# An attention and hard-swish kernel with its weight load moved behind x, some of batch 0's work moved off GpSimd, and a new table of operations

## The chip, the cores and the metric

The kernel runs on one core of one Trainium2 chip. The metric is the device time of a run in microseconds. Five engines take part: TensorE (PE; its weight loads are listed as PEld), VectorE (DVE), ScalarE (ACT), GpSimd (POOL) and SyncE (SP), which here only issues DMAs. Each works through its own list of instructions in order, and waits where an instruction's inputs or its target are not ready.

## The reference

```python
def mab(q, kv):
    s = scale * (q @ kv.transpose(0, 2, 1))
    s = s - s.max(-1, keepdims=True)
    a = np.exp(s)
    a /= a.sum(-1, keepdims=True) + 1e-09
    return a @ kv
h = mab(I, x)            # I: 32 inducing rows, the same for each batch
y = mab(x, h)            # x: 4 x 12480 x 128
...
h = y @ w_in             # 128 x 2048
relu6 = np.clip(h + 3.0, 0.0, 6.0)
return (h * relu6 / 6.0) @ w_out   # 2048 x 128
```

Each batch has two stages. In the first, 32 inducing rows attend over all 12480 rows of x. The second can only begin when that sum over the batch is complete: each row of x attends over the 32 results, and the outcome goes through the two-layer block.

## The kernel before, in words

A batch has six groups of 2048 rows (group numbers 0 to 5; 16 tiles of 128) and a rest of 192 rows (group 6). Everything that the engines do is written out in one string, `ORDER`: a table of 1625 operations, which the loop at L809 turns into calls of the functions `op_...`, one after the other. There is no scheduler behind it: the order of the table, read for one engine, is that engine's list. An entry is a code and its arguments, with the batch and the group first, then tiles or halves, then the PSUM bank (0 to 7), then the engine (V, A, P) where there is a choice. `X.1.2.0.16` loads tiles 0 to 16 of batch 1's group 2.

First stage, for each group: X loads x (1 MB, L422, issued on POOL's queue, into one of five buffers `xr`, so that it waits until the group five before is done with); K casts four tiles to bf16 (L426, four K a group, on ScalarE or VectorE); T transposes eight tiles on TensorE (L432) and Y copies them out of PSUM (L438, VectorE); S makes the logits (L443), E their exponential (L451, ScalarE), A the sum weighted by them (L459, TensorE), H adds it up in `hacc` (L470, L472) and D the denominators in `dacc` (L477, L479).

Between the stages, once a batch: c1 and c2 reduce the denominators (L483, L489), c3 sums them over the partitions with the matrix `ones` (L498, L499), c4 inverts, c5 transposes, c6 writes `HT` (L509); cA and cB make `dH` from it (L529, L532), c7 and c8 a rounded part and its remainder, c9 the two tables `HTs` and `Wd` that the second stage's logits need (L523 to L526). Then comes the two-layer block, evaluated through tables made from the 32 rows and not for each row of x: M multiplies by `w_hi` (L538, 16 times), N squares (L546 on ScalarE; L548 and L549 where it is VectorE's), P multiplies by `w_ob` (L601), G makes the 32 rows exactly with `w_hi` and `w_lo` (L555), cH to cJ, L (L578), cL to cN and cP leave two tables, `BD` and `Cq`.

Second stage, for each group: Z makes the logits, two products into two banks (L624; `Z.b.g.k1.k2` puts the differences in k1 and the logits in k2); Zd and Ze take their exponentials (L634, L639, ScalarE), W spreads one of them over the partitions by DMA (L645, SP's queue); R sums (L653), Rl takes the logarithm (L658, ScalarE), Rz subtracts (L663, VectorE; it reads the logits' bank k2 again), Ra is the exponential of that (L677, ScalarE), Rh a copy in fp16 (L688). Then, for each half group, B expands it into banks 0 to 3 (L696), F takes the exponential of two banks at a time (L706, ScalarE, two F a half), U multiplies (L717, VectorE). For each four tiles l and q sum the result in one of the banks 5 to 7 (L726, L743), v copies it out (L754, VectorE), O stores it (L763, SP's queue).

The weights: wi loads w_in whole (L399), wh rounds a quarter of it to bf16 (`w_hi`, L409), wl subtracts for the remainder (`w_lo`, L412), wo loads w_out (L402, POOL's queue) and wb rounds a quarter of it (`w_ob`, L415). Small things at the start: it loads ScalarE's table of functions, i1 makes the identity (POOL), i6, i7 and i9 are memsets and small copies on POOL (`ones`, `blk`, masks), w.n.k makes n matmuls on zeros (L359). At the end, yb and y0 to y5 compare a few sums with what they must be and leave one flag, which L813 reads; the branch behind it is not taken with these inputs.

The second stage of a batch runs beside the first stage of the next one, interleaved entry by entry in `ORDER`.

Of the kernel before, what the change touches and what calls it, by code (L numbers as in the profile page):

```python
# [28 lines left out]
K.0.2.12.16.V wl.2.P T.0.2.0.8.0 E.0.1.0.16.4 T.0.2.8.16.1 Y.0.2.0.8.0.V A.0.1.0.8.4 wl.3.P D.0.1.V A.0.1.8.16.4
Y.0.2.8.16.1.V S.0.2.0.8.0 K.0.3.0.4.A X.1.0.0.16 H.0.1.4 K.0.3.8.12.A S.0.2.8.16.0 K.0.3.4.8.V K.0.3.12.16.V  # L30
E.0.2.0.16.0 T.0.3.0.8.4 T.0.3.8.16.1 D.0.2.V A.0.2.0.8.0 Y.0.3.0.8.4.V A.0.2.8.16.0 Y.0.3.8.16.1.V S.0.3.0.8.4
K.0.4.0.4.A X.1.1.0.16 H.0.2.0 K.0.4.8.12.A S.0.3.8.16.4 K.0.4.4.8.V K.0.4.12.16.V E.0.3.0.16.4 T.0.4.0.8.0
K.0.6.0.2.A A.0.3.0.8.4 D.0.3.V A.0.3.8.16.4 Y.0.4.0.8.0.V T.0.4.8.16.1 X.1.2.0.16 H.0.3.4 S.0.4.0.8.0 Y.0.4.8.16.1.V
K.0.5.0.4.A T.0.6.0.2.4 K.0.5.8.12.A K.0.5.4.8.V S.0.4.8.16.0 K.0.5.12.16.V T.0.5.0.8.1 E.0.4.0.16.0 Y.0.6.0.2.4.V
T.0.5.8.16.2 Y.0.5.0.8.1.V A.0.4.0.8.4 D.0.4.V A.0.4.8.16.4 Y.0.5.8.16.2.V S.0.5.0.8.1 X.1.3.0.16 S.0.6.0.2.0
E.0.6.0.2.0 H.0.4.4 S.0.5.8.16.1 wb.0.P c2.0.- A.0.6.0.2.4 E.0.5.0.16.1 wb.1.P A.0.5.0.8.1 D.0.5.V wb.2.P A.0.5.8.16.1
wb.3.P c1.0.- X.1.4.0.16 H.0.5.1 c3.0.0 H.0.6.4 c5.0.4 c4.0.0 K.1.0.0.4.A c6.0.4 cA.0.V c7.0.A c9.0.P K.1.0.4.8.A
cB.0.V c8.0.P Z.0.0.4.0 K.1.0.8.12.V K.1.0.12.16.V M.0.0.1 Ze.0.0.0 M.0.1.2 M.0.2.3 N.0.0.1.A N.0.1.2.V Zd.0.0.4
M.0.3.1 N.0.2.3.A R.0.0.4 W.0.0 K.1.1.8.12.V N.0.3.1.A M.0.4.2 K.1.1.12.16.V G.0.0.3 N.0.4.2.A M.0.5.1 G.0.1.3
Rl.0.0.4 N.0.5.1.V M.0.6.2 G.0.2.3 K.1.1.0.4.A M.0.7.4 N.0.6.2.A G.0.3.3 Rz.0.0.0 N.0.7.4.A M.0.8.1 M.0.9.2 N.0.8.1.A  # L40
cH.0.3 P.0.0.4 P.0.1.4 Ra.0.0 M.0.10.0 N.0.9.2.V P.0.2.4 M.0.11.1 N.0.10.0.A P.0.3.4 P.0.4.4 N.0.11.1.A M.0.12.0
P.0.5.4 K.1.1.4.8.A cI.0.3 M.0.13.1 P.0.6.4 N.0.12.0.A M.0.14.2 cJ.0.3 P.0.7.4 N.0.14.2.A M.0.15.0 N.0.13.1.V P.0.8.4
N.0.15.0.A L.0.0.3 P.0.9.4 L.0.1.3 Rh.0.0.V P.0.10.4 cL.0.3 P.0.11.4 P.0.12.4 cM.0.3 P.0.13.4 cN.0.3 P.0.14.4 P.0.15.4
# [35 lines left out]
v.0.5.2.7.V B.1.0.0 q.0.5.3.0.6 cL.1.4 F.1.0.0.0 cM.1.4 F.1.0.0.1 q.0.5.3.1.6 cN.1.4 Z.1.1.0.1 v.0.5.3.6.V T.2.0.0.8.4
Ze.1.1.1 U.1.0.0.2 O.0.5.0.16 l.0.6.0.5 Zd.1.1.0 R.1.1.2 q.0.6.0.0.5 q.0.6.0.1.5 Rl.1.1.2 Y.2.0.0.8.4.V l.1.0.0.7  # L80
q.1.0.0.0.7 Rz.1.1.1 T.2.0.8.16.4 Rh.1.1.V B.1.0.1 Ra.1.1 Y.2.0.8.16.4.V q.1.0.0.1.7 F.1.0.1.0 v.0.6.0.5.V W.1.1
S.2.0.0.8.4 v.1.0.0.7.V S.2.0.8.16.4 l.1.0.1.6 F.1.0.1.1 K.2.2.8.12.V q.1.0.1.0.6 K.2.2.12.16.V q.1.0.1.1.6
# [119 lines left out]
def kernel(  # L202
# [31 lines left out]
    with ExitStack() as es:  # L234
# [53 lines left out]
        w_st = os_[NOS - 1]  # L288
# [109 lines left out]
        def op_wi(e):  # L398
            nc.sync.dma_start(w_st[:, :, :].rearrange("p a c -> p (a c)"), moe_w_in[:, :])  # L399
# [566 lines left out]
```

## Time and profile before

| | us |
|---|---|
| median of 3 runs (lowest, highest) | 324.18 (323.92, 326.12) |
| the profiled execution, its own time | 325.27 |
| its span in the profile | 323.5 |
| mean granted clock of TensorE | 0.94 |

Busy time in that span: TensorE 286.2 us, its weight loads 216.9, VectorE 246.6, ScalarE 225.9, GpSimd 61.0. Time in the rows that follow is counted from the span's start. A row of the timeline has the start, the length, the engine, the line in the kernel, the instruction, output and input, how many in a row, and in brackets how long the engine stood idle before and what ended that. A row of the table of windows has, for one stretch, its length, each engine's busy time with the number of its instructions in brackets, then TensorE's granted clock, the mean busy share of the DMA engines and their GB/s. Matmuls are pipelined, so TensorE counts as busy in part of the time in which it only waits for the next one.

### The profile page before, as it was taken

The numbers are of one execution on the slowest core, as the hardware profiler recorded it, in microseconds if no ns is written. First come the engines' busy times: TensorE is split into PE (matmuls) and PEld (weight loads), VectorE is DVE, ScalarE is ACT, GpSimd is POOL, SyncE is SP. The second block draws the span as 40 slices with busy tenths as digits, with TensorE's granted clock in tenths as the row PEclk, the third lists the DMA queues.
The fourth block names the chain that finished last, engine by engine and source line by source line (L and its number), as shares of the span: only waits on it lengthen the run. The fifth ranks groups of instructions, "written<-read, shape, count | busy, mean of one in ns | idle before, by whom it ended". The sixth has DMA issues, their size and how long they took to land. (4 is left out here: it accounts for less than half of the span.)

```text
span 323.5 us, 9751 instructions
## 1 busy us (share of the span) xinstructions
PE 286.2 (88%) x4101; PEld 216.9 (67%) x4101; DVE 246.6 (76%) x457; ACT 225.9 (70%) x387; POOL 61.0 (19%) x96
## 2 busy tenths in 40 slices
PE   5768399999989999999999998999989996989860
PEld 2567257778767777877877677787767763766640
DVE  2799777999798569889896589999875664877560
ACT  1733286979868788898788789866778677677620
POOL 8452500224221000532420003131110000000000
PEclk9589669999999999999999999999999997899795
DMA  7999820688998047789993338761653248167361
GB/s 235 428 385 363 296 67 3 181 239 237 339 340 308 5 162 232 223 303 344 271 321 135 138 83 257 275 191 28 193 180 138 66 149 256 25 200 219 148 234 56
DMA packets 23462, 66.74 MB, mean 206 GB/s; under 512 B 3664, under 2 KB 16752, under 8 KB 17264
## 3 DMA queue, kind: packets, MB, share of 16 engines
q1 hardware_dynamic: 19216, 39.41, 37.3%
q0 software_dynamic: 4192, 26.61, 24.1%
q8 instruction: 34, 0.56, 0.7%
q14 instruction: 20, 0.16, 0.2%
HBM read 27.67 MB, written 25.56 MB: 165 GB/s over the span
## 5 line engine op out<-in xcount | busy, mean ns | idle before, releaser
L706 ACT ACTIVATE TF<-ps 128x1024 bf16<-128x1024 f32 (+1 forms) x100 | 95.0, 999 | 26.6 <-PE ps L696 26.2
L754 DVE COPY os<-ps 128x512 f32<-128x512 f32 x96 | 64.7, 682 | 16.7 <-PE ps L743 16.3
L717 DVE TENSOR_TENSOR TD<-TF,d 128x2048 bf16<-128x2048 bf16 (+1 forms) x52 | 60.0, 1156 | 13.0 <-ACT TF L706 11.4
L743 PE MATMUL ps<-Cq,TD 128*128 128x128 bf16 (+1 forms) x784 | 60.6, 223 | 1.5 <-DVE TD L717 1.5
L743 PE MATMUL ps<-Cq,TF 128*128 128x128 bf16 (+1 forms) x784 | 61.6, 224 | 0.0
L743 PEld LDWEIGHTS <-TF 128*128 128x128 bf16 (+1 forms) x784 | 46.9, 101 | 14.9 <-issue 11.5
L743 PEld LDWEIGHTS <-TD 128*128 128x128 bf16 (+1 forms) x784 | 48.1, 101 | 7.2 <-issue 3.1
L726 PE MATMUL ps<-BD,a 128*128 128x512 f32 (+1 forms) x100 | 44.4, 462 | 2.0 <-DVE os L754 1.8
L438 DVE COPY xT<-ps 128x1024 bf16<-128x1024 bf16 x48 | 32.6, 683 | 4.6 <-PE ps L432 4.3
L432 PE MATMUL ps<-ident_b,xb 128*128 128x128 bf16 x384 | 30.5, 227 | 6.0 <-ACT xb L426 3.4
L546 ACT ACTIVATE sq<-ps 128x512 bf16<-128x512 f32 x60 | 32.3, 616 | 2.0 <-PE ps L538 1.8
L426 ACT CAST xb<-xr 128x512 bf16<-128x512 f32 x48 | 28.3, 627 | 6.1 <-DMA xr<-in_x_dram 6.1
L479 POOL TENSOR_TENSOR dacc<-dacc,a 128x512 f32<-128x512 f32 x15 | 21.2, 1414 | 59.1 <-ACT a L451 55.3
L432 PEld LDWEIGHTS <-xb 128*128 128x128 bf16 x384 | 24.0, 101 | 11.2 <-issue 4.4
L459 PE MATMUL ps<-xr,a 128*32 128x128 f32 x384 | 29.1, 228 | 2.2 <-ACT a L451 1.5
L459 PEld LDWEIGHTS ps<-xr,a 128*32 128x32 f32 x384 | 24.6, 111 | 4.8 <-ACT a L451 3.5
L426 DVE CAST xb<-xr 128x512 bf16<-128x512 f32 x48 | 24.8, 542 | 3.2 <-DMA xr<-in_x_dram 3.2
L677 ACT ACTIVATE a<-zz 128x512 fp32r<-128x512 f32 (+1 forms) x28 | 16.2, 579 | 14.5 <-DVE z_all L663 11.9
L696 PE MATMUL ps<-z,pair 32*128 32x256 f16 (+1 forms) x400 | 21.7, 275 | 4.2 <-ACT TF L706 2.8
L451 ACT ACTIVATE a<-ps 128x512 fp32r<-128x512 f32 x24 | 14.4, 599 | 14.3 <-PE ps L443 13.3
L726 PEld LDWEIGHTS ps<-BD,a 128*128 128x128 f32 (+1 forms) x100 | 18.0, 188 | 7.2 <-issue 2.6
L538 PE MATMUL ps<-dH,w_hi 128*128 128x512 bf16 x64 | 22.4, 404 | 0.0
(130 smaller groups left out, 371.7 us busy)
## 6 DMA issues: line engine op xcount, KB each, us to landing
xr<-in_x_dram POOLq DMA_DIRECT2D x23, 1024.0 KB, 7.4
out_dram<-os SPq DMA_DIRECT2D x23, 1024.0 KB, 4.8
d<-dk SPq DMA_DIRECT2D x96, 128.0 KB, 3.0
os<-in_moe_w_in_dram SPq DMA_DIRECT2D x1, 1024.0 KB, 4.9
xr<-in_x_dram POOLq DMA_DIRECT2D x2, 512.0 KB, 7.2
w_or<-in_moe_w_out_dram POOLq DMA_DIRECT2D x1, 1024.0 KB, 9.6
out_dram<-os SPq DMA_DIRECT2D x2, 512.0 KB, 4.4
xl<-in_x_dram POOLq DMA_DIRECT2D x4, 96.0 KB, 6.5
```

The lines of the kernel that those rows point to most:

```text
L426: copier(e)(at(xb, xbl, b, g)[:p, lo:hi, :], at(xr, xl, b, g)[:p, lo:hi, :].bitcast(FP32))
L432: nc.tensor.transpose(pt[:, (i - lo) * p : (i - lo + 1) * p], at(xb, xbl, b, g)[:p, i, :], ident_b[:p, :p])
L438: copier(e)(xT_of(b, g)[:, lo * p : hi * p], ps[:, k, :].bitcast(BF16)[:, : (hi - lo) * p])
L459: nc.tensor.matmul(ps[:M, k, :C], lhsT=at(a1, a1l, b, g)[:p, i * M : (i + 1) * M], rhs=at(xr, xl, b, g)[:p, i, :], start=(i == 0), stop=(i ...
L538: nc.tensor.matmul(ps[:, k, :], lhsT=w_hi[:, jb, :], rhs=dH[:, :, :, :, :].rearrange("p q k m i -> p (q k m i)"),)
L546: nc.scalar.activation(sq_of(b, jb)[:, :], ps[:, k, :], ACT.Square)
L696: nc.tensor.matmul(ps[:, j, f * w : (f + 1) * w], lhsT=pair[rows, f].rearrange("p m i -> p (m i)"), rhs=fat(z_, b, g)[rows, h * w : (h + 1 ...
L706: nc.scalar.activation(hat(TF_, b, g, h)[:, 2 * q : 2 * q + 2, :w], ps[:, 2 * q : 2 * q + 2, :w], ACT.Exp, scale=-1.0)
L717: nc.vector.tensor_mul(split(hat(TD_, b, g, h)), split(hat(TF_, b, g, h)), d.unsqueeze(2).to_broadcast([P, n, 2, w]),)
L726: nc.tensor.matmul(ps[:p, k, : J * C], lhsT=fat(a_, b, g)[:rows, s * p : (s + 1) * p], rhs=BD_[b % 2][:rows, :J, :].rearrange("p j c -> p ...
L743: nc.tensor.matmul(ps[:p, k, j * C : (j + 1) * C], lhsT=t[:, j, f * w + s2 * p : f * w + (s2 + 1) * p], rhs=Cq_[b % 2][:, (1 + f) if u els ...
L754: copier(e)(at(os_, osl, b, g)[:p, s * J : (s + 1) * J, :], ps[:p, k, : J * C].rearrange("p (j c) -> p j c", c=C),)
```

## The change

The change replaces the whole table by another of the same 1625 operations, and moves one DMA to another queue.

- wi is issued by POOL and not by SP. In the table it stands behind X.0.5, with wo behind it. x comes first: X.0.0 is the first entry.
- The four wl go from POOL to VectorE and the four wb from POOL to ScalarE. c8 and c9 of batch 0 go from POOL to VectorE; those of batches 1 to 3 stay.
- Of the 100 casts K, ScalarE had 52 and VectorE 48; now ScalarE has 88 and VectorE 12, all twelve of them in batch 0.
- Of the twelve matmuls on zeros, which all stood at the start, eight stay there and four stand behind batch 0's last A.
- i6, which stood in the start, comes behind X.1.1.
- Banks and order are new nearly everywhere. In batch 3's second stage, Z of groups 2 to 6 has its logits in bank 4 and not in bank 0, and the F of a group's second half stand ahead of the next group's Ra and not behind it.
- yb, y0, y4 and y5 stand at the very end.

The new table's beginning, part of its middle, and its end (each line as in the file):

```diff
 ORDER = """
-i0.- it.- X.0.0.0.8 i2.- wi.- w.4.4 X.0.0.8.16 X.0.1.0.16 i1.- w.8.4 X.0.2.0.16 i3.V i8.- X.0.3.0.16 X.0.4.0.16
-K.0.0.0.4.A X.0.6.0.2 K.0.0.4.8.V i6.P wh.1.A wh.0.V i4.4 T.0.0.0.8.0 K.0.0.8.12.A K.0.0.12.16.V i5.4.V wh.3.A
...
-B.3.2.0 U.3.1.1.2 q.3.1.2.0.5 F.3.2.0.0 l.3.1.3.7 v.3.1.1.6.V q.3.1.2.1.5 F.3.2.0.1 Z.3.3.4.0 v.3.1.2.5.V q.3.1.3.0.7
-Ze.3.3.0 U.3.2.0.2 q.3.1.3.1.7 Zd.3.3.4 R.3.3.2 l.3.2.0.6 W.3.3 v.3.1.3.7.V Rl.3.3.2 q.3.2.0.0.6 q.3.2.0.1.6 Rz.3.3.0
-l.3.2.2.5 l.3.2.1.7 Rh.3.3.V B.3.2.1 Ra.3.3 v.3.2.0.6.V q.3.2.1.0.7 F.3.2.1.0 q.3.2.1.1.7 O.3.1.0.16 l.3.2.3.6
...
+X.0.0.0.8 i2.- w.8.3 X.0.0.8.16 X.0.1.0.16 X.0.2.0.16 it.- X.0.3.0.16 K.0.0.0.4.A K.0.0.8.12.A K.0.1.0.4.A i1.- i3.V
+K.0.0.4.8.V X.0.4.0.16 X.0.6.0.2 i8.- K.0.0.12.16.V T.0.0.8.16.4 K.0.1.8.12.A i9.P ia.- Y.0.0.8.16.4.V i0.- i4.0
...
+S.0.2.0.8.0 Y.0.2.8.16.3.V S.0.2.8.16.0 A.0.1.8.16.4 K.0.3.4.8.V X.0.5.0.16 D.0.1.V T.0.3.0.8.3 E.0.2.0.16.0
+A.0.2.0.8.0 A.0.2.8.16.0 wi.- wo.- X.1.0.0.16 K.0.3.8.12.A K.0.3.12.16.V D.0.2.V H.0.1.4 T.0.3.8.16.2 Y.0.3.0.8.3.V
...
+S.0.4.8.16.3 i6.P K.0.5.4.8.V K.0.5.0.4.A T.0.5.0.8.0 c2.0.- H.0.3.2 Y.0.5.8.16.1.V E.0.4.0.16.3 A.0.4.0.8.2
+Y.0.5.0.8.0.V S.0.5.0.8.0 S.0.5.8.16.0 wh.1.V wh.3.V D.0.4.V E.0.5.0.16.0 A.0.4.8.16.2 H.0.4.2 D.0.5.V wh.2.A wl.2.V
+A.0.5.0.8.1 A.0.5.8.16.1 H.0.5.1 wh.0.A c1.0.- w.4.2 wb.2.A wl.1.V H.0.6.4 wb.3.A wb.1.A wb.0.A c3.0.0 c4.0.0 c5.0.2
+X.1.2.0.16 wl.3.V K.1.0.4.8.A K.1.0.0.4.A T.1.0.0.8.3 c6.0.2 c7.0.A wl.0.V K.1.0.12.16.A cA.0.V cB.0.V K.1.0.8.12.A
+K.1.1.0.4.A T.1.0.8.16.4 M.0.1.1 c9.0.V Y.1.0.0.8.3.V N.0.1.1.V K.1.1.8.12.A M.0.8.2 N.0.8.2.A Y.1.0.8.16.4.V i7.P
...
+v.0.0.0.6.V T.1.3.8.16.4 D.1.1.P Y.1.3.8.16.4.V F.0.0.1.0 U.0.0.1.2 q.0.0.1.0.5 q.0.0.1.1.5 v.0.0.1.5.V l.0.0.2.6
+K.1.4.8.12.A B.0.1.0 F.0.1.0.0 F.0.1.0.1 q.0.0.3.0.7 T.1.3.0.8.4 q.0.0.3.1.7 v.0.0.3.7.V Z.0.2.0.1 Ze.0.2.1
...
+l.3.1.2.5 q.3.1.2.0.5 v.3.1.1.6.V F.3.2.0.0 W.3.2 U.3.2.0.2 Z.3.3.3.4 Ze.3.3.4 q.3.1.2.1.5 v.3.1.2.5.V Zd.3.3.3
+l.3.2.0.7 l.3.2.1.6 R.3.3.2 Rl.3.3.2 q.3.2.0.0.7 q.3.2.0.1.7 B.3.2.1 F.3.2.1.0 F.3.2.1.1 Rz.3.3.4 O.3.0.0.16 W.3.3
+q.3.2.1.0.6 q.3.2.1.1.6 l.3.1.3.5 q.3.1.3.0.5 q.3.1.3.1.5 Rh.3.3.V B.3.3.0 Ra.3.3 F.3.3.0.1 F.3.3.0.0 v.3.2.0.7.V
+l.3.2.2.7 q.3.2.2.0.7 v.3.2.1.6.V O.2.6.0.2 l.3.3.0.6 Z.3.4.3.4 Ze.3.4.4 v.3.1.3.5.V O.3.1.0.16 U.3.2.1.2 U.3.3.0.2
...
+B.3.6.0 F.3.6.0.0 O.3.5.0.8 O.3.5.8.16 l.3.6.0.5 yb.0 q.3.6.0.0.5 U.3.6.0.2 q.3.6.0.1.5 v.3.6.0.5.V O.3.6.0.2 y0.0
+y1.- y4.4 y5.4
 """
...
         def op_wi(e):
-            nc.sync.dma_start(w_st[:, :, :].rearrange("p a c -> p (a c)"), moe_w_in[:, :])
+            nc.gpsimd.dma_start(w_st[:, :, :].rearrange("p a c -> p (a c)"), moe_w_in[:, :])
```

More of the change, by code (lines that the diff above doesn't have):

```diff
@@ L29 @@
[L29 to L43, printed above, removed]
@@ L79 @@
[L79 to L82, printed above, removed]
-E.2.0.0.16.4 U.1.0.1.2 B.1.1.0 K.2.2.0.4.A A.2.0.0.8.4 D.2.0.P F.1.1.0.0 A.2.0.8.16.4 v.1.0.1.6.V O.0.6.0.2 l.1.0.2.5
@@ new lines @@
+B.1.1.0 F.1.1.0.1 K.2.2.4.8.A l.1.0.3.5 q.1.0.3.0.5 q.1.0.0.1.7 q.1.0.3.1.5 F.1.1.0.0 Z.1.2.3.2 S.2.1.0.8.4
+S.2.1.8.16.4 Ze.1.2.2 E.2.1.0.16.4 v.1.0.0.7.V v.1.0.1.6.V v.1.0.3.5.V K.2.3.12.16.A U.1.1.0.2 S.2.0.0.8.1
+S.2.0.8.16.1 l.1.1.1.7 l.1.1.0.6 l.1.0.2.5 Zd.1.2.3 R.1.2.4 q.1.0.2.0.5 q.1.1.0.0.6 T.2.2.0.8.3 q.1.1.1.0.7 Rl.1.2.4
+Rz.1.2.2 Rh.1.2.V K.2.3.8.12.A E.2.0.0.16.1 D.2.0.P Ra.1.2 Y.2.2.0.8.3.V T.2.3.8.16.4 Y.2.3.8.16.4.V D.2.1.P
+K.2.3.0.4.A W.1.2 q.1.0.2.1.5 v.1.0.2.5.V q.1.1.1.1.7 v.1.1.1.7.V B.1.1.1 F.1.1.1.1 q.1.1.0.1.6 v.1.1.0.6.V
@@ L171 @@
+Ra.3.6 v.3.5.0.5.V l.3.5.2.7 q.3.5.3.0.6 q.3.5.2.0.7 q.3.5.2.1.7 O.3.4.0.16 v.3.5.2.7.V q.3.5.3.1.6 v.3.5.3.6.V
+B.3.6.0 F.3.6.0.0 O.3.5.0.8 O.3.5.8.16 l.3.6.0.5 yb.0 q.3.6.0.0.5 U.3.6.0.2 q.3.6.0.1.5 v.3.6.0.5.V O.3.6.0.2 y0.0
+y1.- y4.4 y5.4
 """
```

246 lines of the change are left out of this document (124 added, 122 removed).

## The prediction

> **What bounds the kernel now.** I read the table of windows first, cut where batch 0's and the later batches' second stage can begin (HT, L509, written at 37.95, 99.85, 167.05 and 236.10), then the timeline of the start and the chain of waits of the end.
>
> ```profile
> core 0: us, PE busy (x) PEld busy (x) DVE busy (x) ACT busy (x) POOL busy (x), PEclk, DMA share, GB/s
> 0.00:37.95 37.95, 25.32 (x312) 19.32 (x312) 26.85 (x55) 14.14 (x24) 20.12 (x46) 0.83 0.97 351
> 37.95:99.85 61.90, 57.77 (x844) 43.24 (x844) 53.47 (x98) 48.28 (x83) 13.56 (x17) 0.94 0.66 206
> 99.85:167.05 67.20, 66.63 (x1022) 51.45 (x1021) 56.10 (x104) 55.41 (x98) 14.64 (x17) 1.00 0.72 239
> 167.05:236.10 69.05, 67.31 (x1035) 52.16 (x1035) 57.42 (x102) 54.84 (x96) 11.14 (x12) 1.00 0.52 165
> 236.10:314.00 77.90, 69.20 (x893) 50.71 (x890) 52.81 (x99) 53.24 (x89) 1.49 (x4) 0.93 0.48 160
> 314.00:323.50 9.50, 0.00 (x0) 0.00 (x0) 0.00 (x0) 0.00 (x0) 0.00 (x0) 0.57 0.23 76
> ```
> ```profile
> 37.95 0.23 DVE L509 TENSOR_TENSOR HT<-ps,rD 128x64 f32<-128x64 f32 x1
> ```
>
> There are three parts. In the start, 37.95 us, no engine is full: TensorE 25.3, VectorE 26.9, ScalarE 14.1. In the middle, 198.15 us (three rows), one batch's second stage runs beside the next batch's first: TensorE is busy 191.7 (a busy TensorE may still be waiting inside), VectorE 167.0, ScalarE 158.5. In the end, 87.4 us, no first stage is left to fill holes: VectorE and ScalarE are at 53 of 77.9, ahead of a tail of 9.5 us in which no engine works.
>
> **The start.** Three instructions of VectorE are far longer than their like, and each lies beside GpSimd's weight work (w_lo on L412, w_ob on L415):
>
> ```profile
> 8.17 0.62 ACT L426 CAST xb<-xr 128x512 bf16<-128x512 f32 x1 [6.15 <-DMA xr<-in_x_dram]
> ...
> 9.32 2.95 POOL L412 TENSOR_TENSOR w_lo<-os,w_hi 128x512 bf16<-128x512 f32 x2 [0.55 <-DVE w_hi L409]
> 9.43 1.57 DVE L426 CAST xb<-xr 128x512 bf16<-128x512 f32 x1 [0.20 <-DMA xr<-in_x_dram]
> ...
> 17.11 2.78 POOL L412 TENSOR_TENSOR w_lo<-os,w_hi 128x512 bf16<-128x512 f32 x2
> ...
> 17.82 2.69 DVE L426 CAST xb<-xr 128x512 bf16<-128x512 f32 x2
> ...
> 32.40 2.27 POOL L415 CAST w_ob<-w_or 128x512 bf16<-128x512 f32 x4
> ...
> 32.98 2.25 DVE L479 TENSOR_TENSOR dacc<-dacc,a 128x512 f32<-128x512 f32 x1 [0.82 <-ACT a L451]
> ```
>
> Their like, by line (count, then ns as minimum/median/maximum):
>
> ```profile
> L426 ACT CAST xb<-xr x48: 602/620/677, 8.2 to 215.4; 128x512 bf16<-128x512 f32 x48
> L426 DVE CAST xb<-xr x48: 404/416/2357, 8.2 to 217.2; 128x512 bf16<-128x512 f32 x48
> ```
> ```profile
> L479 DVE TENSOR_TENSOR dacc<-dacc,a x5: 681/691/2245, 21.3 to 33.0; 128x512 f32<-128x512 f32 x5
> ```
>
> *w_in behind x.* wi was ahead of everything but I_sb on SP's queue; it goes to POOL's, behind X.0.5. The first casts wait for x until 8.17.
>
> ```profile
> 10.00:12.00 2.00, 1.46 (x16) 0.93 (x16) 2.00 (x4) 1.22 (x2) 2.00 (x2) 0.50 1.07 426
> ```
>
> w_in is 1.05 MB; at 426 GB/s it holds the DMA engines for 2.5 us. I take x as 2.5 us earlier, the far bound, since the first half tile lands while w_in is still owed; the other bound is 0. Late next is w_in itself: POOL issues it after X.0.5, which waits until A.0.0 has freed buffer 0, and wo and X.1.0 stand behind it. Its first reader, wh.1, now comes after group 5's last copy, so the transfer is covered by four groups' work; X.1.0 comes one transfer later, and its casts stand behind the wb on ScalarE. SP loses one issue and waits for nothing new. The Trainium skill ("DMA: Bandwidth & Descriptors", "Anatomy of one DMA — SWDGE (gpsimd) path") has such a transfer cost about 2.0 us and one more for every 436 KB; by that, an estimate, half a tile alone lands 3.2 us after its issue and this term is nearer to -3, the sum half a microsecond lower; no row here has x alone.
>
> *w_lo and w_ob leave GpSimd.* VectorE gets back 1.57 - 0.42, 2.36 - 0.42 and 2.25 - 0.69: 1.15 + 1.94 + 1.56 = 4.6 us (near bound 3, if part of it lay in waits). It pays four subtractions wl: between 0.42 (the one-input cast of this shape) and 1.48 (2.95/2, the same subtraction on GpSimd); I take 0.69, the two-input row, 2.8 us. In the new order wl.2, wl.1, wl.3 and wl.0 stand between the last exponential and cA, wl.3 ahead of c6 and wl.0 ahead of cA. One of them, wl.1, fits into the wait for the denominators' matmuls, so 2.1 stay on the path; at the bounds 1.3 and 5.9. The four wb go to ScalarE at 0.62 each: 2.5 us, covered, since ScalarE is busy 14.14 of 37.95; with that cover gone, +2.5. The memsets of i6 move from the first microseconds to behind X.1.1's wait, beside VectorE's casts: 0 (they read nothing) to 1.15 (the first stretched cast); I take 0. c9 and c8 of batch 0 leave GpSimd too:
>
> ```profile
> 39.83 0.62 PE L624 MATMUL ps<-xT,Wd 128*32 128x512 bf16 x4 [2.14 <-POOL Wd L526]
> ```
>
> TensorE waited 2.14 us for them with the first M in line behind; now M stands ahead of Z and waits for cB alone. Gain 0 to 2.14; wl.0 ahead of cA takes 0.7 back; I count 0.
> Sum: -2.5 - 4.6 + 2.1 = -5: HT at 33. Bounds: 0 - 3 + 5.9 = +3, and -2.5 - 4.6 + 1.3 - 2.1 = -8.
>
> The row 37.95:99.85 has a clock of 0.94: 6% of 61.9, 3.7 us, are lost there, after TensorE had waited in the start. The change moves four of twelve warming matmuls from the beginning to just ahead of c3. If they kept the clock up, the middle would be up to 3.7 shorter; c3, c5 and one transpose stand alone behind them, so I count 0. The Trainium skill ("TensorE: Matmul & The Clock Gate", "Part 1: The HAM clock gate") says that about 3.4 us without work halve the clock and as much sustained work restores it: by that rule the four would help only if no gap behind them reaches 3.4 us, and the time would be 306 instead of the 310 below. The 0.83 and 0.94 above agree that idle costs clock; no row here shows the limit.
>
> **The middle: casts go from VectorE to ScalarE.** All 36 casts K of batches 1 to 3 that VectorE made are ScalarE's in the new table, 35 of them between the first HT and the last (38 stood there, 73 do). ScalarE: 158.5 + 35 x 0.62 = 180 us. VectorE: 167.0 - 36 x 0.42 = 152. At the old length ScalarE is at 180/198 = 91%. How well can it be filled? In its best row above it is at 55.41/67.20 = 82%; in its best ten microseconds:
>
> ```profile
> 60.00:70.00 10.00, 9.35 (x147) 7.18 (x145) 9.20 (x16) 9.20 (x15) 2.43 (x3) 1.00 0.73 209
> ```
>
> At 92% the middle takes 196, 2 less; at 82% it takes 218, 20 more. I take 92%: a cast needs only x, there long before, and the new order puts single casts where ScalarE waits for B (F.0.0.1.0, K.1.4.8.12.A, F.0.1.0.0), which is its largest wait:
>
> ```profile
> ACT TF L706 <- PE ps L696: 26.2, 30, 3.0
> ```
>
> **The end: a bank and an order.** Batch 3's groups follow each other at a fixed pace; Zd of groups 0 and 5 start at
>
> ```profile
> 253.43 0.59 ACT L634 ACTIVATE dk<-ps 128x512 bf16<-128x512 f32 x1
> ...
> 295.16 0.60 ACT L634 ACTIVATE dk<-ps 128x512 bf16<-128x512 f32 x1
> ```
>
> 41.7/5 = 8.35 us a group. One pass in the chain of waits (start, length):
>
> ```profile
> 268.32 0.39 PE ps L653
> 268.73 0.61 ACT ln L658
> 269.36 0.69 DVE zz L663
> 270.09 0.72 ACT a L677 x2
> 270.82 1.83 ACT TF L706 x2
> 272.69 0.61 PE ps L696 x6
> 273.30 3.53 PE ps L743 x32
> ```
>
> R, the logarithm, the subtraction Rz and the exponential Ra stand one behind the other ahead of F. Two things tie them. With Z.3.3.4.0, Rz reads bank 0, which the second half's B (banks 0 to 3) overwrites, so B waits for Rz; and ScalarE's list has Ra, which waits for Rz, ahead of F. The new table has Z.3.3.3.4, so that Rz reads bank 4, outside B's, and the list Rl.3.3, F.3.2.1.0, F.3.2.1.1, Ra.3.3: from group 2 on neither Rz nor Ra stands ahead of F. That takes out 270.82 - 269.36 = 1.46 us a group; B takes their place between Rl and F, at most 0.61, which leaves -0.85; Ra goes into ScalarE's other wait, for the next group's B. The far bound is ScalarE's own list, four F of 0.92, three reads of 0.61 and Ra 0.72: 6.2 us, -2.1 a group. I take -1.2, six groups: -7. Bounds 0 (another engine or ring holds the pace) and -13.
> y0, y4 and y5 now follow the last copy: seven short instructions of at most 0.23 (HT's row, 64 columns wide) make 1.6 us, beside the last output's landing; I take 0.
>
> **Sum.** 325.27 in the profiled execution (span 323.5 and 1.8 around it) - 5 - 2 - 7 = 311.3; the median shown, 324.18, is 1.1 lower, so 310.
>
> **The rivals.**
> *ScalarE becomes the bound (slower).* The 35 casts do not fill waits but push F, Ra and the squares back, and TensorE, 191.7 of 198 already, waits for each. Against it: VectorE, at 9.20 of 10 above, is freed by nearly as much. At ScalarE's best stage, 82%: +20 - 5 - 7 = +8, 332. It decides below 86% (180 / 210, where the 12 us of start and end are used up).
> *Only the start.* The rings or VectorE hold the end's pace and the middle stays: -5, 319. For it: U and the copies stand in the same cycle.
> *ScalarE at 95%.* 180/0.95 = 189.5, -8.5 in the middle: 304. Against it: no stretch above reaches it.
> *No earlier start.* x did not wait for w_in and the subtractions eat what GpSimd gives back: 315.
>
> **How the numbers follow.** Forecast 310: 0.48. 95%, 304: 0.17 (the rule on the clock lies in it). Only the start, 319: 0.17. ScalarE bound, 332: 0.12. No earlier start, 315: 0.06. The likeliest one's own range is 305 to 315. For eight in ten the range leaves out the slower case and the far bounds: 299 to 322. About 1%, 320.9 to 327.4, is what a measurement here can tell from no change. Faster: 0.48 + 0.17 + 0.06 + 0.10 of the start-only case, 0.81; slower 0.11, the ScalarE case less its near edge; same 0.08.
>
> **What would show it.** First casts near 5.7, HT near 33, no instruction of VectorE above 1.2 us in the start; ScalarE near 180 between the first and the last HT, and that stretch near 196; Zd of batch 3 every 7.2 us. A middle above 205 with TensorE waiting for TF or xb, or an HT after 37, would prove it wrong.

## The result, and the profile after

| | before | after |
|---|---|---|
| median (lowest, highest), us | 324.05 (323.76, 326.12) | 309.33 (307.8, 310.61) |
| the profiled execution, its own time | 325.27 | 308.12 |
| its span | 323.5 | 306.3 |

The ratio is 0.9528, 95% interval 0.9469 to 0.9588. A second measurement of the same kernel gave 0.9481 (0.9435 to 0.9527). The kernel before took 325.69, 325.79 and 326.23 us (medians) beside the three groups of experiments further down, so kernels of different groups are compared by their ratios to it. Runs over 1.5% above the fastest of their kernel are in the medians but not in the ratios: two of four with the weights' work back on GpSimd, one of four of the kernel after once more, one of five with later loads of x.

The table of windows of the kernel after, cut at the same four instructions (HT at 33.32, 98.34, 169.22 and 232.33), has these rows; the columns are those of the table of before.

```profile
0.00:33.32 33.32, 24.68 (x318) 19.50 (x320) 24.82 (x59) 17.06 (x29) 12.36 (x39) 1.00 0.96 362
33.32:98.34 65.02, 59.09 (x864) 44.90 (x863) 50.35 (x90) 56.04 (x98) 10.28 (x11) 0.92 0.60 191
98.34:169.22 70.88, 67.42 (x1043) 53.67 (x1043) 53.39 (x93) 60.94 (x110) 13.95 (x17) 0.98 0.73 242
169.22:232.33 63.11, 62.54 (x979) 49.50 (x979) 50.96 (x91) 59.09 (x105) 11.24 (x14) 1.00 0.57 182
232.33:299.00 66.67, 63.66 (x902) 47.25 (x902) 54.53 (x100) 51.43 (x87) 3.44 (x4) 1.00 0.61 202
299.00:306.30 7.30, 0.00 (x0) 0.00 (x0) 0.00 (x0) 0.00 (x0) 0.00 (x0) 0.58 0.05 13
```

| part | before | after | difference | forecast |
|---|---|---|---|---|
| start | 37.95 | 33.32 | -4.6 | -5 |
| middle | 198.15 | 199.01 | +0.9 | -2 |
| end | 87.40 | 73.97 | -13.4 | -7 |
| sum | 323.5 | 306.3 | -17.2 | -14 |

The total is close to the forecast, but two of its three parts are not: the middle got nothing where 2 us were expected, and the end got twice what was expected.

**The start.** The timeline of VectorE shows the first cast and the last stretch before the block (start, length, line, operation):

```profile
6.04 0.43 DVE L426 CAST xb<-xr 128x512 bf16<-128x512 f32 x1 [0.80 <-DMA xr<-in_x_dram]
...
30.97 0.99 DVE L412 TENSOR_TENSOR w_lo<-os,w_hi 128x512 bf16<-128x512 f32 x1
31.89 0.27 DVE L472 TENSOR_TENSOR hacc<-hacc,ps 32x128 f32<-32x128 f32 x1
32.09 0.34 DVE L502 RECIPROCAL rD<-ps 128x32 f32<-128x32 f32 x1
32.35 0.12 DVE L503 COPY d_all<-ps 128x32 f32<-128x32 f32 x1
32.40 0.99 DVE L412 TENSOR_TENSOR w_lo<-os,w_hi 128x512 bf16<-128x512 f32 x1
33.32 0.20 DVE L509 TENSOR_TENSOR HT<-ps,rD 128x64 f32<-128x64 f32 x1
33.45 0.99 DVE L412 TENSOR_TENSOR w_lo<-os,w_hi 128x512 bf16<-128x512 f32 x1
34.37 0.56 DVE L529 TENSOR_TENSOR dH<-HT 128x256 bf16<-128x256 f32 x1
```

No row has a bracket from 30.97 on, so VectorE has no wait there. Three subtractions w_lo stand ahead of HT (the first at 28.91) and the fourth ahead of dH; each takes 0.99 us and not the 0.69 of the forecast. What they cost HT is measured below.

**The middle.** At the head of VectorE's list of waits in the middle stands one that took 1.5 us there before (line, what it waited for, us in total, times, longest):

```profile
DVE TD L717 <- DMA d<-dk: 8.1, 3, 3.4
```

U multiplies by `d`, which W spreads over the partitions by DMA. Around the first of the two long stops the windows read:

```profile
66.00:70.00 4.00, 4.00 (x63) 2.83 (x60) 2.44 (x3) 3.99 (x7) 1.26 (x1) 1.00 0.92 233
70.00:74.00 4.00, 1.13 (x14) 0.70 (x14) 1.48 (x2) 2.10 (x5) 0.00 (x0) 1.00 1.00 392
74.00:78.00 4.00, 4.00 (x49) 3.45 (x47) 2.66 (x6) 2.55 (x4) 0.00 (x0) 0.60 0.95 370
```

TensorE works 1.13 of 4 us while the DMA engines are full (share 1.00), and behind the stop its clock is 0.60. The chain of waits (start, length) and the timelines of GpSimd and VectorE name the parties:

```profile
66.44 5.96 DMA d<-dk
...
152.80 8.40 DMA d<-dk
```
```profile
65.27 0.55 POOL L422 DMA_DIRECT2D xr<-in_x_dram  x1 [7.54 <-PE ps L459]
```
```profile
72.52 1.23 DVE L717 TENSOR_TENSOR TD<-TF,d 128x2048 bf16<-128x2048 bf16 x1 [3.18 <-DMA d<-dk]
```

A load of x (X.2.0, 1 MB) was issued at 65.27, in the middle of W.0.2's pieces, and the piece that U waited for took 5.96 us to land, where the page's section on DMA issues has 3.0 as the median of these 128 KB pieces. The second stop has X.3.1 and X.3.2 (152.51 and 154.36) beside W.1.4, whose piece takes 8.40 us. Stores of outputs, 1 MB each, stand in SP's queue near both pieces too (issued at 67.14, and from 143.92 on).

**The end.** Zd of batch 3's groups 0 and 5, from the timeline of ScalarE:

```profile
241.02 0.60 ACT L634 ACTIVATE dk<-ps 128x512 bf16<-128x512 f32 x1
...
281.86 0.62 ACT L634 ACTIVATE dk<-ps 128x512 bf16<-128x512 f32 x1
```

From group 2 (261.15) on they follow each other every 6.5 to 6.9 us, and the list of TensorE's waits is empty between them. In the kernel before they did not come at a fixed pace, as the prediction reads them, but 11.3, 3.3, 11.9, 7.9, 7.3 and 10.4 us apart (groups 0 to 6). Seven microseconds of the new cycle in the windows:

```profile
267.00:274.00 7.00, 6.99 (x98) 4.99 (x102) 6.40 (x10) 6.10 (x10) 0.00 (x0) 1.00 0.67 205
```

By busy time TensorE is the engine at its limit there, with 6.99 of 7.00 us; VectorE has 6.40 and ScalarE 6.10.

### The profile page after: what moved, and what is told of

It reads as the page before. It is cut to its first block, busy times and chain, and to the rows that moved or that the text cites. A ratio compares the mean times of both kernels' runs of the same rounds, so it can differ in the third digit from the quotient of the medians.

```text
span 306.3 us, 9742 instructions
## 1 busy us (share of the span) xinstructions
PE 277.4 (91%) x4093; PEld 214.8 (70%) x4101; DVE 234.0 (76%) x429; ACT 244.6 (80%) x427; POOL 51.3 (17%) x85
## 4 chain that ended last, share of the span: by engine, by line
PE 73%; DVE 11%; DMA 8%; ACT 2%; issue 2%; SPq 2%; DVEq 0%; ACTq 0%; POOLq 0%
PE ps L743 26%; PE ps L726 8%; PE ps L432 6%; PE ps L459 5%; PE ps L601 5%; PE ps L696 5%; DMA d<-dk 5%; PE ps L538 5%; PE ps L624 4%; DVE TD L717 3%; PE ps L443 2%; PE ps L653 2%; DVE xT L438 2%; PE ps L555 2%; DMA xr<-in_x_dram 2%
## 5 line engine op out<-in xcount | busy, mean ns | idle before, releaser
L717 DVE TENSOR_TENSOR TD<-TF,d 128x2048 bf16<-128x2048 bf16 (+1 forms) x52 | 63.1, 1220 | 11.2 <-DMA d<-dk 8.1
L743 PE MATMUL ps<-Cq,TD 128*128 128x128 bf16 (+1 forms) x784 | 58.8, 220 | 3.7 <-DVE TD L717 3.7
L426 ACT CAST xb<-xr 128x512 bf16<-128x512 f32 x84 | 50.4, 624 | 7.1 <-DMA xr<-in_x_dram 7.0
L743 PEld LDWEIGHTS <-TD 128*128 128x128 bf16 (+1 forms) x784 | 46.9, 99 | 10.4 <-DVE TD L717 5.3
L726 PE MATMUL ps<-BD,a 128*128 128x512 f32 (+1 forms) x100 | 42.3, 462 | 0.0
L432 PE MATMUL ps<-ident_b,xb 128*128 128x128 bf16 x384 | 32.1, 235 | 5.4 <-DVE fac L393 3.2
L459 PE MATMUL ps<-xr,a 128*32 128x128 f32 x384 | 31.7, 236 | 0.5 <-ACT a L451 0.5
L459 PEld LDWEIGHTS ps<-xr,a 128*32 128x32 f32 x384 | 27.1, 116 | 3.6 <-issue 1.3
L422 POOL DMA_DIRECT2D xr<-in_x_dram x25 | 14.1, 566 | 77.9 <-PE ps L459 33.0
L663 DVE CUSTOM_DVE_ANT_0 zz<-ln,ps 128x512 f32<-128x512 f32 (+1 forms) x28 | 17.3, 619 | 8.1 <-ACT ln L658 7.8
L538 PE MATMUL ps<-dH,w_hi 128*128 128x512 bf16 x57 | 20.8, 402 | 0.4 <-ACT sq L546 0.2
```

The source lines that it names most:

```text
L426: copier(e)(at(xb, xbl, b, g)[:p, lo:hi, :], at(xr, xl, b, g)[:p, lo:hi, :].bitcast(FP32))
L432: nc.tensor.transpose(pt[:, (i - lo) * p : (i - lo + 1) * p], at(xb, xbl, b, g)[:p, i, :], ident_b[:p, :p])
L459: nc.tensor.matmul(ps[:M, k, :C], lhsT=at(a1, a1l, b, g)[:p, i * M : (i + 1) * M], rhs=at(xr, xl, b, g)[:p, i, :], start=(i == 0), stop=(i ...
L538: nc.tensor.matmul(ps[:, k, :], lhsT=w_hi[:, jb, :], rhs=dH[:, :, :, :, :].rearrange("p q k m i -> p (q k m i)"),)
L717: nc.vector.tensor_mul(split(hat(TD_, b, g, h)), split(hat(TF_, b, g, h)), d.unsqueeze(2).to_broadcast([P, n, 2, w]),)
L726: nc.tensor.matmul(ps[:p, k, : J * C], lhsT=fat(a_, b, g)[:rows, s * p : (s + 1) * p], rhs=BD_[b % 2][:rows, :J, :].rearrange("p j c -> p ...
```

## The experiments

The theory: x first and the weights off GpSimd give the start; the casts give the middle something that the late `d` takes away; the bank and the order of F and Ra give the end. The rivals: ScalarE is now the bound and the casts cost time; the subtractions cost the start more than GpSimd did; the end's gain comes from the new order as a whole and not from the bank. In the first four kernels below the line numbers are three lower than in the kernel after.

**x behind w_in again.** wi goes back to SP's queue, ahead of X.0.0.

```diff
+wi.- X.0.0.0.8 i2.- w.8.3
...
-A.0.2.0.8.0 A.0.2.8.16.0 wi.- wo.- X.1.0.0.16
+A.0.2.0.8.0 A.0.2.8.16.0 wo.- X.1.0.0.16
```

> The changed kernel with one thing undone: w_in is loaded first, on SP's queue, as before. If x waited for w_in (the prediction's first term, 2.5 us), the first casts start near 8.2 and not at 6.0, HT of batch 0 comes at 35.5 to 36 and not at 33.3, and the run takes about 311.8 us. If the start is held by VectorE's own work (the rival), the first casts are late as well but HT moves by less than 1 us, and the time stays within 1 us of 309.3.

Measured: 313.02 us, ratio 0.9591 (0.9536 to 0.9647). VectorE's first cast of x:

```profile
8.30 0.43 DVE L423 CAST xb<-xr 128x512 bf16<-128x512 f32 x1 [3.05 <-DMA xr<-in_x_dram]
```

It comes 2.26 us later (8.30 against 6.04; 5.65 and 5.70 in two other kernels with the same start), HT 1.4 later (34.73 against 33.32). In the eight profiles with x first and the subtractions in place HT lies between 32.56 and 33.57, so 1.2 to 2.2 us reach the end of the start. So x did wait for w_in. The rest of the difference between the two profiled executions lies mostly in the middle, where VectorE waited 10.5 us for `d` and not 8.1; since the kernel after itself, run once more, has 5.3 there, that part is not shown to come from the edit.

**The weights' work back on GpSimd.** wl, wb and batch 0's c8 and c9.

```diff
-wl.2.V
+wl.2.P
...
-wb.2.A
+wb.2.P
...
-c9.0.V
+c9.0.P
```

> The changed kernel with w_lo's subtractions, w_ob's casts and batch 0's c8 and c9 back on GpSimd, at the same places in the table. If GpSimd's work stretches VectorE's (the prediction's second term), VectorE has single instructions of 1.5 us and more beside it again and HT moves by the net of the two, about +2 us: 35.3, and the run takes 311.4 us. If the four subtractions, which measured 1.0 us each on VectorE and stand on the path, cost as much as the stretching (the rival), HT stays at 33 or comes up to 1.5 us earlier, and the time is 308 to 309.5 us. The table's first M may come later in both, since Wd and HTs come from GpSimd again.

Measured: 312.07 us, ratio 0.9501 (0.9414 to 0.9589), which is no difference from the kernel after (0.9528), and HT at 31.43, 1.9 us earlier than after and not later. The rival on the subtractions is right as far as HT goes. No gain shows in the time; in the profiled execution (314.55 us) VectorE waits 12.4 us for `d` in the middle. The same edit is tried again below without the late `d`.

**The casts back.** Of the casts K of batches 1 to 3, the 36 of tiles 8 to 16 go back to VectorE.

```diff
-K.1.0.8.12.A
+K.1.0.8.12.V
...
-K.1.0.12.16.A
+K.1.0.12.16.V
```

> The changed kernel with the 36 casts of batches 1 to 3 back on VectorE, each at its new place in the table. The middle, from the first HT to the last, was 199.0 us. If moving the casts was worth the predicted 2 us, it becomes 201, and the run 311.3 us. If ScalarE, busy 176 of 199, holds the middle (first rival), it becomes shorter: 193 to 196, the run 303 to 306. If late DMAs hold it, W's above all (second rival), both stops of VectorE for d stay and the middle moves by less than 1 us.

Measured: 315.78 us, ratio 0.9685 (0.9607 to 0.9764). The three stages of the middle are 66.67, 73.01 and 65.08, each about 2 us longer than after. The kernel after, run once more, has 66.15, 71.45 and 63.09, so only the third stage is clear of the spread between executions; the time of the whole run is clear of it too (0.9481 and 0.9528 for the kernel after). So in the new order the casts are worth time on ScalarE, and ScalarE as the new bound is refuted.

**Bank 0 again.** In batch 3's groups 2 to 6 the logits go to bank 0, and Rz stands behind Rl (it must read bank 0 ahead of B); group 3 as the example:

```diff
-Z.3.3.3.4 Ze.3.3.4 ... Zd.3.3.3 ... Rl.3.3.2 ... F.3.2.1.1 Rz.3.3.4
+Z.3.3.4.0 Ze.3.3.0 ... Zd.3.3.4 ... Rl.3.3.2 Rz.3.3.0 ... F.3.2.1.1
```

> The changed kernel with the logits of batch 3's groups 2 to 6 in bank 0 again, as before (and the differences in bank 4), Rz right behind Rl in the table, which leaves VectorE's order as it is. If B then waits for Rz and this held the end's pace (the prediction's third term, first half), each of the five groups takes 0.7 us more: from the last HT to the end 77.5 us and not 74.0, Zd every 7.5 us and not every 6.8, the run 312.8 us. If the bank does not matter and the order on ScalarE alone does (rival), the end stays within 0.5 us.

Measured: 316.22 us, ratio 0.9691 (0.9614 to 0.9769). The end is 80.13 us against 73.97, more than the 77.5 expected, and TensorE has this wait again (240 to 290 us; 3.9 us in five times over the whole end):

```profile
PE ps L693 <- DVE z_all L660: 2.4, 3, 1.4
```

The bank is worth about 6 us. B waits for Rz, as the mechanism said; besides, Z, which now writes a bank that F still reads, waits 1.0 us for F. TensorE's idle time from the last HT to the last copy goes from 0.9 us to 5.8.

**The same bank and order in the kernel before.** Groups 2 to 6 of batch 3 get bank 4 and have Ra behind the F of the half before. The first l of groups 4 to 6, which stood ahead of those F, goes behind Ra, whose result it reads, and R of group 5 gives bank 4 up for bank 2; group 3 as the example:

```diff
-Z.3.3.4.0 ... Rz.3.3.0 ... B.3.2.1 Ra.3.3 ... F.3.2.1.1 v.3.2.1.7.V l.3.3.0.7 B.3.3.0
+Z.3.3.3.4 ... Rz.3.3.4 ... B.3.2.1 ... F.3.2.1.1 Ra.3.3 v.3.2.1.7.V l.3.3.0.7 B.3.3.0
```

> The kernel before with one thing of the change added: in batch 3's groups 2 to 6 the logits lie in bank 4 (the differences in bank 3) and Ra stands behind the two F of the second half before it. Everything else is as before. If these two made the end shorter (the prediction's third term), the end goes from 87.4 us to 80.4 (the predicted -7) or further, and the run takes 317 us; the four other stages stay. If the end gained for another reason, from the order of the table part and of groups 0 and 1 or from the tail (rival), it stays above 85 us and the run above 321.

Measured: 330.77 us, ratio 1.0161 (1.0107 to 1.0214): slower. The end is 91.5 us, above the 85 of the rival. TensorE's waits from HT to 306:

```profile
PE ps L726 <- ACT a L677: 5.9, 3, 2.6
PE ps L624 <- ACT TF L706: 2.0, 3, 0.7
PE ps L696 <- ACT TF L706: 1.6, 2, 1.0
```

The first wait is new, and the one for Rz is gone. With Ra moved back, l comes right behind it; TensorE stands in l with B behind it, and the wait for Rz has become one for Ra. Bank and order are no gain by themselves: TensorE's own list has to change with them, which the new table does (B.3.3.0 stands ahead of Ra.3.3 there, and l.3.3.0 well behind it).

**The kernel after, once more,** on the chip of the next two.

> The changed kernel itself, unchanged, as the measure for the others of this call. All theories: stages of 33.3 us, 65 to 68, 71 to 74, 63 and 74, and 308 to 312 us.

Measured: 309.69 us, ratio 0.9481 (0.9435 to 0.9527).

**Two ways to get `d` in time.** First, two stores of outputs go behind W on SP's queue:

```diff
-K.1.5.0.4.A O.0.0.0.16 ... W.0.3
+K.1.5.0.4.A ... W.0.3 O.0.0.0.16
...
-q.1.3.1.1.6 O.1.2.0.16 ... W.1.4
+q.1.3.1.1.6 ... W.1.4 O.1.2.0.16
```

> The changed kernel with two stores moved in SP's queue: O.0.0 behind W.0.3, O.1.2 behind W.1.4. In the changed kernel VectorE stood still for d twice in the middle, 3.2 and 3.4 us, with d landing 6 and 8.4 us after its issue. If the stores of the same queue make d late, both stops shrink below 1.5 us, the first two stages of the middle lose 3 to 6 us (62 to 63 and 67 to 69) and the run takes 303 to 307 us. If the loads of x beside them do (rival), the stops stay above 2 us and the time within 2 us of the unchanged kernel.

Measured: 308.93 us, ratio 0.9458 (0.9426 to 0.9489): no difference in time from the kernel after. But the trace does not clear the stores. The stop for `d` near 161 is gone and the second stage is 68.47 us (70.88, and 71.45 in the kernel after once more); the first stop is still 2.21 us (with the stores at their old places and the loads too, six profiles have 2.9 to 4.9 at the first and 2.2 to 6.1 at the second). And a new one follows it: the copy at 80.75 waits 4.02 us for the store that was moved back, and the first stage is 67.70. What the edit gains at one stop it loses at another. Second, three loads of x are issued later:

```diff
-A.1.1.8.16.4 X.2.0.0.16 H.1.1.4
+A.1.1.8.16.4 H.1.1.4
...
-D.1.2.P F.0.3.0.0
+D.1.2.P X.2.0.0.16 F.0.3.0.0
...
-A.2.2.8.16.4 X.3.1.0.16 H.2.2.4 ... X.3.2.0.16 ... D.2.4.P
+A.2.2.8.16.4 H.2.2.4 ... D.2.4.P X.3.1.0.16 X.3.2.0.16
```

> The changed kernel with three loads moved in GpSimd's queue: X.2.0 behind D.1.2, X.3.1 and X.3.2 behind D.2.4, so that they are issued 4 to 6 us later and not beside W.0.2 and W.1.4. If the loads of x make d late, both stops for d shrink below 1.5 us and the first two stages of the middle lose 3 to 6 us; the run takes 303 to 307 us. If the stores make it late, nothing changes by more than 2 us; if x then comes late itself, a wait of K for xr takes the place of the one for d.

Measured: 302.98 us, ratio 0.9281 (0.9247 to 0.9316): this beats both kernels, by 6 to 7 us against the kernel after on the same chip. Its windows of the three stages of the middle, and of the 4 us that were empty before:

```profile
33.43:94.28 60.85, 57.85 (x865) 43.72 (x863) 49.27 (x91) 56.02 (x98) 10.34 (x11) 0.94 0.64 204
94.28:161.50 67.22, 66.27 (x1044) 52.25 (x1042) 54.79 (x93) 60.01 (x107) 13.91 (x17) 1.00 0.73 235
161.50:225.72 64.22, 63.00 (x983) 49.63 (x980) 50.97 (x90) 59.91 (x106) 11.34 (x14) 1.00 0.62 202
```
```profile
70.00:74.00 4.00, 4.00 (x64) 3.31 (x63) 3.59 (x7) 3.79 (x9) 0.00 (x0) 1.00 1.00 299
```

The middle is 192.29 us, VectorE's wait for `d` there is down to 0.6, and TensorE is busy 187.1 of it. With the stores at their old places, later loads of x remove both stops, so they are what delayed W at the first. At the second either edit alone removes the stop: there loads and stores together made W late.

The last four kernels start from this one, so that no late `d` covers what is tested.

**The weights on GpSimd, without the late `d`.** The edit of the second experiment.

> The later loads of x kept, and the weights' work (wl, wb, c8 and c9 of batch 0) back on GpSimd. If the four subtractions of 1.00 us on VectorE are what holds the start, HT comes near 31.4 instead of 33.4 and, with no late d to eat it, the time is about 301 against 303. If GpSimd's slower pass only shifts the loss behind HT (w_lo and w_ob late for the block, casts stretched), the first stage of the middle is longer than 60.9 by the same 2 us or more: 303 to 306.

Measured: 304.2 us, ratio 0.9309 (0.927 to 0.9347), which overlaps with 0.9281 (0.9247 to 0.9316). HT is at 31.43 again, 2.0 earlier, and the first stage of the middle is 64.95 us against 60.85, as the second expectation has it. GpSimd begins the weights' work only at 28.83, behind the casts of x, so that it stretches neither these nor the additions. What takes the gain back in the profile is in TensorE's timeline:

```profile
33.59 1.00 PE L538 MATMUL ps<-dH,w_hi 128*128 128x512 bf16 x2
38.88 0.62 PE L624 MATMUL ps<-xT,Wd 128*32 128x512 bf16 x4 [4.30 <-POOL Wd L526]
```

c9 stands behind all of wl and wb on GpSimd, Z waits 4.30 us for it, and all but two M stand behind Z. That c9 alone on VectorE would keep the 2 us was not tried.

**The subtractions behind M.** wl stays on VectorE but goes behind Y.1.1.0.8, c8.0, Rz.0.0 and N.0.9.

```diff
-wl.2.V A.0.5.0.8.1
+A.0.5.0.8.1
...
-c7.0.A wl.0.V K.1.0.12.16.A
+c7.0.A K.1.0.12.16.A
...
-N.0.9.0.V T.1.1.8.16.4
+N.0.9.0.V wl.0.V T.1.1.8.16.4
```

> The later loads of x kept, and the four subtractions wl left on VectorE but moved behind the first M, where VectorE has waits. If all four lie on the path to M, as VectorE's list without a gap from 24 to 39 us says, HT comes at 31.5 and the first M 3 us earlier, and the time is 300 to 301. If something else (the casts of x, the matrix products of the rows) is late next, HT moves but the time stays at 303.

Measured: 306.41 us, ratio 0.9403 (0.9371 to 0.9436): slower by 3.4 us in the medians. HT comes at 31.08 as expected, but TensorE meets the late w_lo in G:

```profile
46.09 0.21 PE L555 MATMUL ps<-HTb,w_lo 128*128 128x32 bf16 x1 [2.75 <-DVE w_lo L412]
```

Neither expectation holds: the next to be late was G, which was left where it stood. That the subtractions lie on the path to HT is shown; that they can be hidden is not, since G was not moved with them.

**The casts back, without the late `d`.** The edit of the third experiment.

> The later loads of x kept, and 36 casts of batches 1 to 3 back on VectorE. The forecast's term for the middle, 2 us for the whole of it, gives 305. The differences in the kernel with casts back and the loads as they were, about 2 us a stage, give 309. If the casts were worth nothing by themselves, 303.

Measured: 307.6 us, ratio 0.9425 (0.9399 to 0.9451): 4.6 us slower than with the casts on ScalarE. The stages are 63.73, 69.20 and 66.11, each longer by 1.9 to 2.9. What the casts cost on VectorE is in TensorE's waits of the middle, first with the casts on ScalarE, then with 36 of them back on VectorE:

```profile
PE ps L432 <- ACT xb L426: 1.3, 1, 1.3
```
```profile
PE ps L432 <- DVE xb L426: 5.2, 3, 2.1
```

The transposes T wait 3.9 us longer for their casts, and F, which needs TensorE's B, waits 19.2 us in ScalarE's list and not 7.3.

**Ra ahead of F, bank 4 kept.**

```diff
-Rl.3.3.2 ... B.3.2.1 F.3.2.1.0 F.3.2.1.1 Rz.3.3.4 ... Ra.3.3
+Rl.3.3.2 Rz.3.3.4 ... B.3.2.1 Ra.3.3 F.3.2.1.0 F.3.2.1.1
```

> The later loads of x kept, and in batch 3 Rz right behind Rl and Ra ahead of the F of the half before, with the logits still in bank 4. If the bank alone is what counts (B no longer waits for Rz and TensorE stays full at 6.9 us a group), the time is 303. If the order of ScalarE's list counts as much, F waits for Rz and Ra again, up to 1.3 us a group, and the time is 306 to 310.

Measured: 306.3 us, ratio 0.9404 (0.9368 to 0.9439): 3.3 us slower. The end is 78.39 us against 73.48, Zd of groups 3 to 6 come 7.2 to 8.4 us apart, and ScalarE waits for Rz again:

```profile
ACT a L677 <- DVE z_all L663: 6.3, 6, 1.6
```

The bank alone is not enough either: the order of Rz and Ra is worth another 3 us.

## Why the prediction came out right, step by step

**The start: total right, -4.6 against -5; two of its steps wrong.** "I take x as 2.5 us earlier": the first cast came 2.1 to 2.5 earlier, but by the first experiment only 1.2 to 2.2 count at HT. The far bound was taken for the value. "VectorE gets back 1.57 - 0.42, 2.36 - 0.42 and 2.25 - 0.69", 4.6 us, was the right effect with the wrong cause. The stretched instructions are gone (no single one of VectorE in the start is above 1.01 us), but they are also gone with the work still on GpSimd, because the new table puts it behind the casts. "I take 0.69, the two-input row": it measured 0.99. That row's inputs are both f32 and read without gaps; w_lo has a bf16 input and reads w_in at every 16th column, as the cast w_hi does, which takes 0.60 on VectorE where the casts of x take 0.42. No run separates the two. Three of the four stand ahead of HT, so the move itself cost about 2 us at HT (31.43 with the work on GpSimd) where the forecast had it gain 2.5. c8 and c9, counted at 0, probably gave that back: with all of the work on GpSimd TensorE waits 4.30 us for c9, but they were not moved by themselves. Between the kernels with and without the whole move the runs cannot tell (304.2 and 302.98), so the rival "no earlier start" was right that the subtractions eat what GpSimd gives back, and wrong that x had not waited for w_in.

**The middle: -2 forecast, +0.9 measured; a wait was missed.** In the new order the casts are worth 4.6 us, more than the 2; what they are worth in the old one was not measured. The late `d`, two stops with the slow clock behind them, took 6 to 7 back. The step that failed is "Late next is w_in itself": of the transfers only those of the start were followed, and X of the later batches, "new nearly everywhere" in the new table, were not set against W. The 92% for ScalarE came out (without the stops it is busy 175.9 of 192.3 us, 91.5%), but it does not set the length alone: TensorE is busy 187.1 of the same 192.3. The forecast's reason, that casts fill ScalarE's waits for B, fits the runs: these waits are 7.3 us with the casts there and 19.2 without. (The 26.2 us that the prediction shows for them are those of the whole execution; the middle has 16.8.) What it did not name is that TensorE's transposes wait for casts on VectorE, 5.2 us against 1.3. ScalarE's wait for Rz, 7.1 us in the middle of the kernel before, is no part of the casts' worth: it is 0.2 with the later loads and still 0.4 with the casts back, so the rest of the new order removed it.

**The end: -7 forecast, -13.4 measured; the waits as priced, the clock left out.** From the last HT to the last copy out of PSUM (behind it come another 9.6 us in both kernels; the rows above begin the tail at 314 and 299, that is 0.1 and 2.3 us behind that copy):

| | before | after |
|---|---|---|
| length | 77.8 | 64.4 |
| TensorE busy (matmuls) | 69.2 (893) | 63.5 (900) |
| TensorE idle | 8.6 | 0.9 |
| granted clock | 0.93 | 1.00 |

TensorE's idle time falls by 7.7 us, near the forecast's 7, and nearly the same number of matmuls takes 5.7 us less. The clock accounts for most of that: 69.2 us at 0.93 are 64.4 at 1.00, an estimate from these rows. The prediction prices the clock only in the middle; in its own row for the end it stands at 0.93, and the forecast of the end has no term for it. The measured -13.4 lies just beyond its bound of -13.

Undone one at a time in the new table, the bank brings back 4.9 us of that idle time and the order 2.9 (5.8 and 3.8 us against 0.9). The agreement of the 7.7 with the 7 is partly luck all the same. By the measure that the prediction names, Zd of groups 0 and 5, the pace hardly changed (8.35 us a group before, 8.17 after), since Zd of group 0 now comes far earlier. By group 1 to group 6 (264.70 to 305.57, and 254.75 to 288.34) it is 40.9 and 33.6 us; by the multiplication U of the second half of groups 1 to 5 (276.62 to 310.24, and 265.16 to 292.03) it is 33.6 and 26.9: 1.5 to 1.7 us a group and not 1.2, over five groups and not six. The clock is in these figures too. Two more things were off. "The far bound is ScalarE's own list", 6.2 us a group: the engine that was reached first is TensorE, with 6.9. And the price assumed that TensorE's list allows the new order; in the old table it does not, and the same edit costs 5 us there. Both halves of the mechanism, bank and order, are shown by the runs above, each taken out of the new table alone.

The middle's miss of 3 us and the end's surplus of 6 stand against each other; that the median came within 1 us of the forecast is luck.

**The rivals.** ScalarE as the bound: refuted by both kernels with casts back. Only the start: refuted, the end is 13.4 us shorter. ScalarE at 95%: not reached, with 88.5% of the middle in the kernel after and 91.5% with the later loads. No earlier start: half right, as said above. The warming matmuls: with the later loads of x they end at 30.0 us, TensorE's clock is 0.50 from 34 to 40 us, and the first stage of the middle has 0.94, as before the change. They kept nothing that shows; no run leaves them out.

## What to carry to other kernels

An order of operations has one list for each engine, and an edit that frees one of them pays only if the list of the engine at the bound lets it: taken out of the new table, the bank cost 6 us and the order 3, and both put into the old one cost 5. Where an engine must wait for a small DMA, look at which large loads and stores are issued within the few microseconds around it, and issue those later if nothing waits for them: the later loads gained 6 us, a later store only moved the wait. A total that comes out as forecast says little about the steps: cut both profiles at the same instructions and compare part by part.

## What the runs showed of the hardware

**The clock falls on short waits.** In the kernel before, TensorE had no wait above 1.27 us between 268 and 273, yet (windows of one microsecond):

```profile
268.00:269.00 1.00, 0.92 (x4) 0.47 (x4) 0.37 (x1) 0.89 (x3) 0.00 (x0) 1.00 0.89 219
269.00:270.00 1.00, 0.00 (x0) 0.00 (x0) 0.64 (x2) 0.33 (x1) 0.00 (x0) 1.00 1.04 400
270.00:271.00 1.00, 0.40 (x8) 0.20 (x8) 0.48 (x3) 0.91 (x3) 0.00 (x0) 0.97 1.01 418
271.00:272.00 1.00, 0.22 (x2) 0.10 (x2) 0.00 (x0) 1.00 (x2) 0.00 (x0) 0.50 0.87 324
...
277.00:278.00 1.00, 1.00 (x17) 0.70 (x9) 1.00 (x2) 0.59 (x1) 0.00 (x0) 0.62 0.00 0
278.00:279.00 1.00, 1.00 (x16) 0.67 (x17) 0.52 (x2) 1.00 (x2) 0.00 (x0) 1.00 0.00 0
```

The clock is halved from 271 to about 277.7. The work from 273.2 on ran at half speed, so a stretch with three short waits (1.19, 1.27 and 0.52 us) cost about another 2 us, an estimate from these rows. In the kernel after, one wait of 2.87 us was followed by the slow clock from about 74.9 on (0.50 in the microsecond from 75), and one of 3.26 us, up to 163.11, by 0.50 in the microsecond from 164. TensorE's timeline has these waits, in the kernel before and after:

```profile
270.11 0.40 PE L696 MATMUL ps<-z,pair 32*128 32x256 f16 x8 [1.19 <-DVE z_all L663]
271.78 0.39 PE L696 MATMUL ps<-z,pair 32*128 32x256 f16 x2 [1.27 <-ACT TF L706]
272.69 0.61 PE L696 MATMUL ps<-z,pair 32*128 32x256 f16 x6 [0.52 <-ACT TF L706]
```
```profile
73.80 0.62 PE L743 MATMUL ps<-Cq,TD 128*128 128x128 bf16 x8 [2.87 <-DVE TD L717]
```

The Trainium skill ("TensorE: Matmul & The Clock Gate", "Part 1: The HAM clock gate") puts about 3.4 us without work ahead of the slow clock. Both cases differ from that: the waits were shorter, and in the first case broken by work. A low share of work over a few microseconds was enough here.

**A small transfer beside large ones.** The 128 KB pieces of `d` take 3.0 us in the median, and took 5.96 and 8.40 where one or two loads of 1 MB were issued within 2 us of them (one 1.2 us ahead of the first piece; one 0.3 ahead of the second and one 1.6 behind). With these loads issued later, VectorE's stops of 3.18 and 3.36 us are gone. Output stores of the same size count too: with two of them behind W on SP's queue the second stop is gone although the loads stayed.

**Two inputs beside GpSimd.** With the weights' work on GpSimd, the two subtractions dH (L529, L532) took 0.92 and 1.00 us instead of 0.56 and 0.57, while the copy out of PSUM next to them kept its length:

```profile
31.69 0.92 DVE L529 TENSOR_TENSOR dH<-HT 128x256 bf16<-128x256 f32 x1
32.53 1.00 DVE L532 TENSOR_TENSOR dH<-HT 128x256 bf16<-128x256 f32 x1
33.45 0.68 DVE L438 COPY xT<-ps 128x1024 bf16<-128x1024 bf16 x1
```

The Trainium skill ("SBUF — State Buffer", "SBUF: two separate sides") has an instruction of VectorE with two inputs in SBUF share a pair of ports with GpSimd, one of them waiting for the other; the rows agree with that.
